# Loading the keys in 256-byte pieces with one PSUM copy per head pair, and issuing a step's V gathers in two halves

## The chip, the core and the metric

The kernel runs on one core of a Trainium2 chip. A core has a matrix engine (TensorE, PE in the profile, with its weight loads shown as PEld), a vector engine (DVE), a scalar engine (ACT), a general engine (POOL) and a sync engine (SP) that computes nothing and issues DMAs. Data lie in HBM, in the on-chip SBUF (128 partitions) and in PSUM, where matmuls write. Sixteen DMA engines move data between HBM and SBUF. Each engine works through its own instruction list in order and waits on semaphores for the others.

The metric is the device time of one launch in microseconds (us). Three executions of the kernel before took 688.04, 689.6 and 687.48 us; the median is 688.04 us.

## The reference

A block-sparse attention (BigBird) feeds a mixture-of-experts layer. B=4 sequences, H=8 heads, S=768 tokens, D=64, blocks of 32 tokens, all float32.

```
scores = q @ k.T / sqrt(D)
mask   = |block_i - block_j| <= 1, or block_i or block_j is first or last,
         or block_j is one of three sampled blocks of block_i
attn   = softmax(where(mask, scores, -1e9)) ; x = attn @ v      # x: 3072 rows of 512
logits = normalize(x) @ normalize(expert_emb).T / tau           # 8 experts
e      = argmax(logits) ; gate = softmax(logits)[e]
out    = gate * (relu(x @ w1[e]) @ w2[e])                       # 512 -> 1024 -> 512
```

## The kernel before

The attention works on chunks of 128 queries of one sequence, 24 in all. Two sequences are handled side by side: chunks 0 to 11 belong to sequences 0 and 1, chunks 12 to 23 to sequences 2 and 3. The loop `for s in range(NCH + 1)` (line 1326) has 25 steps. Step `s` scores chunk `now`, prepares chunk `after`, weighs the values of chunk `last` and turns the output of chunk `past`. The order is written out by hand: every engine receives its instructions in the order of this loop and runs them in that order, so a late instruction holds back everything behind it on its engine.

**Keys.** There are 16 head pairs `g`, four per sequence. `load_k` (line 419) loads one pair, 384 KB. Partition p holds six consecutive tokens of each of the two heads, so one piece of the DMA is 6 x 64 x 4 = 1536 bytes, and one DMA covers the pair. `turn_k` (line 492) turns a pair into the transposed layout `kt` with six TensorE transposes into a PSUM tile `kps` (line 501; a transpose takes two tokens of one head side by side) and four copies to `kt` (line 507), each of 64 partitions x 384 elements, two on DVE and two on ACT. The copies write every second token column. The PSUM pool `big` has two buffers; the score tiles `ac`, `dps` and `bps` use the same two. Pairs 0 to 3 are turned before step 0, pairs 4 to 7 at the end of step 1, pairs 8 to 15 in steps 10, 11 and 12 (table `turning`). In those three steps the copies of sampled key blocks into `kg` (`gather_k`, lines 536 and 540) come after the turned keys. SBUF has six buffers for raw keys; the table `keys_at` says in which step pairs 8 to 15 are loaded.

**Values.** Each chunk needs the V rows of its sampled blocks. `gather_v` (line 462) issues one DMA per sampled block and query block: 12 for a pair of chunks (two sequences side by side), each of 32 rows x 16 heads x 256 bytes, into one of two ring buffers `vg`. They are read by `weigh_far` (line 659). The loads of whole V blocks (`vt`) follow the table `values_at`.

**Queries.** `load_q` (line 410) loads 128 queries of two sequences (512 KB in 256-byte pieces) into one of two buffers; `turn_q` (line 513) transposes one chunk's part.

**SP's queue.** `fetch_all` (line 471) issues the gathers of a step, with one ordinary load ahead of every second gather (line 475 the loads, 477 the gathers), and the loads that remain behind them (479). Rows of finished outputs are written to HBM from the same queue (line 820, `x_dram<-x`), at the start of a later step; the next use of that one of three `x` buffers, in `normalize` (line 698), waits for the write to land. Eight semaphores serve the DMAs of SP and ACT in turn, so an issue waits for the landing of the DMA eight places before it.

After the attention, 25 expert tiles of 128 rows follow (`expert_tile`, lines 1157 and 1170), with the weights loaded by line 1110.

Of the kernel before, what the change touches and what calls it, by code (L numbers as in the profile page):

```python
# [3 lines left out]

# [1 line left out]

# [6 lines left out]
F32 = mybir.dt.float32  # L13
# [7 lines left out]
P = 128  # L21
B, H, S, D = 4, 8, 768, 64
# [3 lines left out]
NC = S // P  # L26
# [28 lines left out]
NS = NCH // DUO  # L55
# [316 lines left out]
def shifts(k, engine, s, c):  # L372

    blocks = blocks_of(c)
    key = engine, s, c
    if key not in k.shift:
        _, values = k.nc.values_load_multi_w_load_instructions(
            k.offset[0:1, s, NG * c + blocks[0]:NG * c + blocks[-1] + 1], engines=(engine,), min_val=0, max_val=S - BLK,
            skip_runtime_bounds_check_because="the block numbers are clamped to the blocks there are")
        if engine == mybir.EngineType.SP and s == NRAND - 1:  # L380
            return list(values)
        k.shift[key] = list(values)
    return k.shift[key]


def pair_chunk(s):

    a, at = divmod(s, NC)
    return a, at if a == 0 else (at + 1) % NC


def place(n):

    a, c = pair_chunk(n // DUO)
    return DUO * a + n % DUO, c, n % DUO


def of_seq(src, a, i=None):

    if i is None:  # L400
        return src[DUO * a:DUO * (a + 1)].rearrange("i h s d -> s (i h) d")
    return src[DUO * a + i].rearrange("h s d -> s h d")


def in_pair(t, i=None):

    return t.rearrange("p i h e -> p (i h) e") if i is None else t[:, i]
# [11 lines left out]
def load_k(k, g):  # L419

    b, j = divmod(g, NPAIR)
    k.raw["k", g] = t = k.kld.tile([P, 2, NC, D], F32, name="kraw", tag="kraw", bufs=6)
    return [(t.rearrange("p h c d -> p h (c d)"), k.k[b, 2 * j:2 * j + 2].rearrange("h (p c) d -> p h (c d)", p=P))]


def load_v(k, a, m, i=None):

    v, src = in_pair(k.vt[m], i), of_seq(k.v, a, i)
    return [(v[rows, :, 0:D], src[lo:lo + rows.stop - rows.start]) for rows, lo in pieces(m)]
# [7 lines left out]
def stack(k, s, i=None):  # L437

    st, (_, c) = k.st_ring[s % 2], pair_chunk(s)
    for half in (1,) if c == 0 else (0, 1):  # L440
        k.nc.scalar.copy(out=st[0:D, half, which(i)], in_=k.vt[c][D * half:D * (half + 1), which(i)])


def stack_ends(k, s, halves, i=None):

    for half in halves:
        k.nc.gpsimd.tensor_copy(out=k.st_ring[s % 2][D:P, half, which(i)], in_=k.vt[0][0:D, which(i)])


def blocks_of(c):  # L450

    return range(2 if c == 0 else 0, NG)
# [9 lines left out]
def gather_v(k, s, i=None):  # L462

    a, c = pair_chunk(s)
    t, src = k.vg_ring[s % 2], of_seq(k.v, a, i)
    for r in range(NRAND):
        for g, shift in zip(blocks_of(c), shifts(k, mybir.EngineType.SP, r, c)):
            yield in_pair(t[r * BLK:(r + 1) * BLK, g], i)[:, :, 0:D], src[bass.ds(shift, BLK)]
# [23 lines left out]
def turn_k(k, g):  # L492

    nc = k.nc
    b, j = divmod(g, NPAIR)
    kt = k.kt[b % 2]
    raw = k.raw.pop(("k", g))
    ps = k.big.tile([P, 2, 512], F32, name="kps", tag="big")
    for h in range(2):
        for m in range(NC // 2):  # L500
            nc.tensor.transpose(ps[:, h, m * P:(m + 1) * P], raw[:, h, 2 * m:2 * m + 2].rearrange("p e d -> p (e d)"),  # L501
                                k.ident)
    for h in range(2):
        to = kt[D * h:D * (h + 1), j, 0:S].rearrange("r (p m e) -> r e m p", m=NC // 2, e=2)
        for e in range(2):
            copy = nc.vector.tensor_copy if e == h else nc.scalar.copy
            copy(out=to[:, e], in_=ps[D * e:D * (e + 1), h, 0:3 * P].rearrange("r (m p) -> r m p", m=NC // 2))  # L507
    if j == NPAIR - 1:
        for i, block in enumerate((NB - 1, 0)):
            nc.scalar.copy(out=kt[:, :, S + i * BLK:S + (i + 1) * BLK], in_=kt[:, :, block * BLK:(block + 1) * BLK])  # L510
# [738 lines left out]
def attention_fast(n, ctx):  # L1249
# [3 lines left out]
    nc = n.nc  # L1253
# [65 lines left out]
    nc.sync.dma_start(n.x_dram[N:N + 1, :], zero)  # L1319

    turning = {10: (8, 9), 11: (10, 11, 12), 12: (13, 14, 15)}
    keys_at = {3: (8,), 4: (9,), 5: (10,), 6: (11,), 7: (12,), 8: (13,), 10: (14, 15)}
    values_at = {7: (0,), 8: (1,), 9: (2,), 11: (3,), 13: (4,), 15: (5,)}
    routed = {TURNS.index(DUO * b + 1) + 2: b for b in range(NS - 1)}
    plan = []
    for s in range(NCH + 1):
        now, after, last, past = (TURNS[i] if 0 <= i < NCH else None for i in (s, s + 1, s - 1, s - 2))
        if s in routed:
            plan = after_step(n, routed[s]) + [p for p in plan if p[0] >= s]

        def planned(half):
            for when, part, what in plan:
                if (when, part) == (s, half):
                    what()

        def keys_gathered():
            if after is not None:
                gather_k(n, after)

        ends = last is not None and place(last)[1] == 0  # L1340
        late_keys = s == 1 or s in turning
        if now is not None:
            score_near(n, now)
            score_far(n, now)
        if not late_keys:
            keys_gathered()
        planned(0)
        if s == 0:
            stack_ends(n, 1, (0, 1), 0)
            stack(n, 1, 0)  # L1350
            near_v(n, 1, range(NG), 0)
        elif s == 2:
            stack_ends(n, 0, (1,), 1)
            stack(n, 0, 1)
            near_v(n, 0, range(NG), 1)
        elif s == 3:
            stack_ends(n, 1, (0, 1), 1)
            stack(n, 1, 1)
            near_v(n, 1, range(NG), 1)
        elif s == 4:  # L1360
            stack_ends(n, 0, (0,))
            stack(n, 2)
        elif s % 2 and 5 <= s < NCH:
            if s // DUO + 1 in (NC, NC + 1):
                stack_ends(n, s // DUO + 1, (0, 1))
            stack(n, s // DUO + 1)
        if last is not None:
            weigh_near(n, last, 0)
        if ends:
            score_ends(n, last, 0)  # L1370
            score_ends(n, last, 2)
        if past is not None:
            turn_x(n, past)
        for g in turning.get(s, ()):
            turn_k(n, g)
        if s in turning:
            keys_gathered()
        for part in range(2):
            if last is not None:
                weigh_far(n, last, part)  # L1380
            if after is not None and part == 0 and not ends:
                turn_q(n, after)
        if ends:
            weigh_ends(n, last, (0, 2))
            score_ends(n, last, 1)
            score_ends(n, last, 3)
            if after is not None:
                turn_q(n, after)
        if past is not None:
            chunk_logits(n, past)  # L1390
        ahead, odd = s // DUO + 1, s % DUO
        loads, gathers = [], ()
        if s in (2, 3):
            loads += load_q(n, s)
        elif s >= 4 and not odd and ahead + 1 < NS:
            loads += load_q(n, ahead + 1)
        if s == 3 or s >= 4 and not odd and ahead < NS:
            gathers = gather_v(n, ahead)
        if s == 3:
            near_v(n, 2, (0, 1))  # L1400
        elif s == 4:
            near_v(n, 2, (2, 3))
            near_v(n, 3, (0, 1))
        elif s > 4 and ahead < NS:
            near_v(n, ahead, (2, 3) if odd else (0, 1))
        for g in keys_at.get(s, ()):
            loads += load_k(n, g)
        for m in values_at.get(s, ()):
            loads += load_v(n, 1, m)
        fetch_all(n, gathers, loads)  # L1410
        if ends:
            weigh_ends(n, last, (1, 3))
        if last is not None:
            weigh_near(n, last, 1)
            normalize(n, last)
        if s == 0:
            build_consts(n)
            next(experts)
        if s == 1:
            for g in range(NPAIR, 2 * NPAIR):  # L1420
                turn_k(n, g)
            keys_gathered()
            next(experts)
            next(experts)
            setup.close()
            n.dp = pool("dp_e", 1)
        if s == NC * (B - 1):
            right.close()
            n.wp = n.wp_ctx.enter_context(n.tc.tile_pool(name="wp", bufs=1, side="right", reuse_waits="tile"))
        planned(1)  # L1430
# [224 lines left out]
```

## Time and profile before

| what | value |
|---|---|
| median of three executions | 688.04 us |
| the profiled execution's own time | 691.25 us |
| its span | 689.5 us |
| mean granted TensorE clock | 0.953 |
| start of step 4, 6, 8 (first score matmul) | 90.58, 107.17, 123.77 us |
| start of step 9, 10, 11, 12, 13 | 141.23, 150.67, 165.95, 188.39, 210.57 us |
| first expert matmul (line 1157) | 322.34 us |
| PE busy | 620.6 us (90%) |
| DMA packets | 166,864, of them 123,176 under 512 bytes |

Times inside the execution are counted from the span's start. The span is what the profile covers; the execution's own time is 1.75 us longer, and 3.2 us above the median of the runs. A group's line gives the source line, engine, operation, output and inputs, shape, count, busy time and mean time of one, then the idle time of the engine before them and what ended most of it. The chain is followed back from the last instruction, at each place to what released it; only work on the chain can shorten the execution directly. The granted clock is 1.00 when TensorE runs at full speed, and it drops in stretches where TensorE idles.

### The profile page before, as it was taken

To read this page: it belongs to the slowest core of one execution; us is meant where nothing else is said; L and a number is where in the kernel's file an instruction comes from. 1 tells how busy PE (TensorE), PEld (TensorE's weight loads), DVE (VectorE), ACT (ScalarE), POOL (GpSimd) and SP (SyncE) were. 2 spreads that over 40 slices of the span, in tenths; PEclk is the share of its full clock that TensorE was granted. 3 is DMA by queue.
4 is the path that set the end of the run, shared out by engine and by line. 5 is a ranking of instruction groups with operands and counts; after the bars stand their busy time and mean duration, and the time that the engine had idled before them with its cause. 6 is when DMAs were issued, how large, how long until landed. Compare 5 with 4: busy or idle time off the path is not lost.

```text
span 689.5 us, 18383 instructions
## 1 busy us (share of the span) xinstructions
PE 620.6 (90%) x7496; PEld 483.9 (70%) x7496; DVE 254.0 (37%) x764; ACT 162.1 (24%) x310; POOL 245.2 (36%) x472
## 2 busy tenths in 40 slices
PE   5493999696677999999999999999999999999996
PEld 3382898596577888888777667766477664776673
DVE  3625456344536667723392111121211212112110
ACT  2434455343544554443000000000000000000000
POOL 1321836253208555412202324432344223442232
PEclk9995999888678999999999999999999999999998
DMA  8972479999529999623999999999899998999811
GB/s 207 190 156 50 90 129 177 187 164 204 73 66 138 142 195 165 166 65 119 392 397 402 401 398 405 366 334 344 314 367 412 391 402 317 375 414 388 315 47 32
DMA packets 166864, 170.58 MB, mean 247 GB/s; under 512 B 123176, under 2 KB 127400, under 8 KB 163954
## 3 DMA queue, kind: packets, MB, share of 16 engines
q1 hardware_dynamic: 159458, 155.35, 77.4%
q0 software_dynamic: 5216, 13.43, 5.4%
q8 instruction: 61, 1.00, 0.7%
q10 hardware_dynamic: 2096, 0.52, 0.4%
q14 instruction: 33, 0.27, 0.1%
HBM read 156.65 MB, written 12.90 MB: 246 GB/s over the span
## 4 chain that ended last, share of the span: by engine, by line
PE 76%; DVE 8%; ACT 5%; DMA 2%; issue 2%; SPq 1%; POOL 0%; DVEq 0%; POOLq 0%; ACTq 0%
PE hp L1157 23%; PE yp L1170 22%; PE av L634 7%; PE dps L579 5%; PE ac L554 3%; PE yp L722 3%; PE ac L557 3%; ACT kt L507 3%; DVE kt L507 2%; PE hp L1202 2%; PE yp L1222 2%; PE xg_ps L518 2%; DMA w<-in_moe_w_dram 2%; DVE xt L713 2%; PE xg_ps L711 1%
## 5 line engine op out<-in xcount | busy, mean ns | idle before, releaser
L1157 PEld LDWEIGHTS hp<-xgt,w 128*128 128x128 f32 x1472 | 167.8, 192 | 11.5 <-issue 10.2
L1157 PE MATMUL hp<-xgt,w 128*128 128x128 f32 x1472 | 169.2, 275 | 0.9 <-DMA w<-in_moe_w_dram 0.9
L1170 PE MATMUL yp<-w,h 128*128 128x512 f32 x368 | 161.9, 592 | 0.0
L1170 PEld LDWEIGHTS yp<-w,h 128*128 128x128 f32 x368 | 68.1, 190 | 76.5 <-issue 75.8
L1081 POOL DMA_INDIRECT xg<-x_dram,quarter x88 | 89.4, 1016 | 32.3 <-issue 27.4
L1160 ACT ACTIVATE h<-hp 128x512 f32<-128x512 f32 x23 | 13.7, 597 | 284.1 <-PE hp L1157 240.4
L1183 POOL DMA_INDIRECT out_dram<-y,slot_l x20 | 20.5, 1026 | 155.8 <-DVE y L1182 155.8
L536 POOL COPY kg<-kt 128x128 f32 x176 | 43.9, 296 | 85.1 <-DVE kt L507 78.6
L1164 DVE TENSOR_SCALAR h<-hp 128x512 f32<-128x512 f32 x23 | 15.9, 691 | 148.3 <-PE hp L1157 148.3
L554 PE MATMUL ac<-qt,kt 128*64 128x128 f32 x352 | 52.1, 309 | 16.5 <-DVE qt L523 14.5
L489 POOL COPY vg<-vt 32x1040 f32<-32x1040 f32 (+1 forms) x45 | 43.1, 957 | 60.5 <-PE av L634 48.4
L554 PEld LDWEIGHTS ac<-qt,kt 128*64 128x64 f32 x352 | 46.1, 159 | 17.8 <-issue 15.7
L557 PE MATMUL ac<-qt,kt 128*64 128x256 f32 (+1 forms) x192 | 51.6, 422 | 3.2 <-ACT kt L510 3.2
L579 PEld LDWEIGHTS dps<-qt,kg 128*64 128x64 f32 x1408 | 50.7, 147 | 2.4 <-issue 2.4
L579 PE MATMUL dps<-qt,kg 128*64 128x64 f32 x1408 | 49.1, 231 | 2.0 <-DVE kg L536 2.0
L1182 DVE TENSOR_SCALAR y<-yp,gate 128x512 f32<-128x512 f32 x20 | 15.0, 750 | 82.0 <-PE yp L1170 69.9
L523 DVE COPY qt<-xg_ps 64x512 f32<-64x512 f32 x48 | 33.1, 689 | 30.7 <-PE xg_ps L518 30.3
L584 ACT ACTIVATE pd<-dps,bias 128x256 f32<-128x256 f32 x88 | 34.7, 475 | 20.2 <-PE dps L579 20.2
L634 PE MATMUL av<-st,pac 128*64 128x65 f32 x704 | 32.0, 233 | 7.0 <-DVE x L811 5.7
L507 DVE COPY kt<-kps 64x384 f32<-64x384 f32 x32 | 26.8, 838 | 29.3 <-ACT kt L507 28.9
L507 ACT COPY kt<-kps 64x384 f32<-64x384 f32 x32 | 26.6, 832 | 29.0 <-DVE kt L507 28.6
L501 PE MATMUL kps<-ident,kraw 128*128 128x128 f32 x96 | 17.7, 341 | 16.6 <-issue 16.6
(229 smaller groups left out, 686.8 us busy)
## 6 DMA issues: line engine op xcount, KB each, us to landing
w<-in_moe_w_dram SPq DMA_DIRECT2D x52, 2048.0 KB
vg<-in_v_dram SPq DMA_DIRECT2D x114, 128.0 KB
kraw<-in_k_dram SPq DMA_DIRECT2D x16, 384.0 KB
x_dram<-x SPq DMA_DIRECT2D x10, 516.0 KB
qraw<-in_q_dram SPq DMA_DIRECT2D x9, 512.0 KB
w<-in_moe_w_dram SPq DMA_DIRECT2D x8, 512.0 KB
vt<-in_v_dram SPq DMA_DIRECT2D x10, 256.0 KB
vt<-in_v_dram SPq DMA_DIRECT2D x5, 512.0 KB
```

The costliest lines, as they stand in the source:

```text
L489: k.nc.gpsimd.tensor_copy(out=k.vg_ring[s % 2][NRAND * BLK:P, g, which(i)], in_=k.vt[m][rows, which(i)])
L507: copy(out=to[:, e], in_=ps[D * e:D * (e + 1), h, 0:3 * P].rearrange("r (m p) -> r m p", m=NC // 2))
L523: k.nc.vector.tensor_copy(out=t[rows, :, h], in_=ps[rows])
L536: copy(out=t[:, :, g, s * BLK:(s + 1) * BLK], in_=kt[:, :, bass.ds(shift, BLK)])
L554: nc.tensor.matmul(out[0:D, j, half], lhsT=kt[:, j, at:at + D], rhs=qt[:, j, :, D * half:D * (half + 1)], start=True, stop=True)
L557: nc.tensor.matmul(out[D:P, j, half:2].rearrange("p f h t -> p h f t"), lhsT=kt[:, j, S:S + D], rhs=qt[:, j, :, D * half:P].rearrange("p h ...
L579: nc.tensor.matmul(out[D * r:D * (r + 1), NG * j + g], lhsT=kg[:, j, g, D * r:D * (r + 1)], rhs=qt[:, j, :, cols], start=True, stop=True)
L584: nc.scalar.activation(e[:, :, g].rearrange("p j h t -> p j (h t)"), out.rearrange("p (j g) h t -> p j g (h t)", g=NG)[:, :, g], ACT.Exp, ...
L634: k.nc.tensor.matmul(av[lanes, h // NPAIR, h % NPAIR * P:h % NPAIR * P + D + 1], lhsT=lhsT, rhs=rhs, start=first[0], stop=last, skip_group ...
L1081: k.nc.gpsimd.indirect_dma_start(out=x[:, g], out_offset=None, in_=quarters, in_offset=bass.IndirectOffsetOnAxis(ap=k.quarter[:, g, t:t + ...
L1157: nc.tensor.matmul(hp[:, f, :], lhsT=w1[:, d, (f0 + f) * P:(f0 + f + 1) * P], rhs=xt[:, d, :], start=(d == 0), stop=(d == ND - 1))
L1170: nc.tensor.matmul(yp, lhsT=h[:, f, :], rhs=w2[:, f, :], start=(f == 0), stop=(f == NF - 1))
```

## The change

A pair of K is loaded by two DMAs, one per head, so that partition p holds tokens p, 128 + p, 256 + p and so on. One piece is then one token of one head, 256 bytes. `turn_k` transposes the two heads of a 128-token chunk together, and the columns arrive in the order that `kt` wants; one copy of 128 partitions x 768 elements replaces the four, on DVE for even and on ACT for odd pairs. The table of K loads starts at step 2 with two pairs and goes on with one per step from 3 to 6; pairs 14 and 15 stay in step 10. From step 4 on an even step issues the first six gathers and the odd step after it the other six; the load of queries moves from the even to the odd step. Step 3's gathers stay whole.

```diff
 def load_k(k, g):
-    k.raw["k", g] = t = k.kld.tile([P, 2, NC, D], F32, name="kraw", tag="kraw", bufs=6)
-    return [(t.rearrange("p h c d -> p h (c d)"), k.k[b, 2 * j:2 * j + 2].rearrange("h (p c) d -> p h (c d)", p=P))]
+    k.raw["k", g] = t = k.kld.tile([P, NC, 2, D], F32, name="kraw", tag="kraw", bufs=6)
+    return [(t[:, :, h], k.k[b, 2 * j + h].rearrange("(c p) d -> p c d", p=P)) for h in range(2)]
...
 def turn_k(k, g):
-    for h in range(2):
-        for m in range(NC // 2):
-            nc.tensor.transpose(ps[:, h, m * P:(m + 1) * P], raw[:, h, 2 * m:2 * m + 2].rearrange("p e d -> p (e d)"),
-                                k.ident)
-    for h in range(2):
-        to = kt[D * h:D * (h + 1), j, 0:S].rearrange("r (p m e) -> r e m p", m=NC // 2, e=2)
-        for e in range(2):
-            copy = nc.vector.tensor_copy if e == h else nc.scalar.copy
-            copy(out=to[:, e], in_=ps[D * e:D * (e + 1), h, 0:3 * P].rearrange("r (m p) -> r m p", m=NC // 2))
+    for c in range(NC):
+        nc.tensor.transpose(ps[:, c // 3, c % 3 * P:(c % 3 + 1) * P], raw[:, c].rearrange("p h d -> p (h d)"), k.ident)
+    copy = nc.scalar.copy if g % 2 else nc.vector.tensor_copy
+    copy(out=kt[:, j, 0:S].rearrange("p (w t) -> p w t", w=2), in_=ps[:, :, 0:3 * P])
...
-    keys_at = {3: (8,), 4: (9,), 5: (10,), 6: (11,), 7: (12,), 8: (13,), 10: (14, 15)}
+    keys_at = {2: (8, 9), 3: (10,), 4: (11,), 5: (12,), 6: (13,), 10: (14, 15)}
...
-        elif s >= 4 and not odd and ahead + 1 < NS:
+        elif s >= 4 and odd and ahead + 1 < NS:
             loads += load_q(n, ahead + 1)
-        if s == 3 or s >= 4 and not odd and ahead < NS:
+        if s == 3:
             gathers = gather_v(n, ahead)
+        elif s >= 4 and ahead < NS:
+            if not odd:
+                coming = gather_v(n, ahead)
+            gathers = coming if odd else islice(coming, 6)
```

More of the change, by code (lines that the diff above doesn't have):

```diff
@@ L2 @@
 from functools import partial
-from itertools import zip_longest
+from itertools import islice
 import dataclasses
```

## The prediction

> **What bounds the kernel now.** I read the chain that ended last first, then the groups, then the chain in order of time, then clock and DMA by stretch, then SP's own queue.
>
> ```profile
> PE 76%; DVE 8%; ACT 5%; DMA 2%; issue 2%; SPq 1%; POOL 0%; DVEq 0%; POOLq 0%; ACTq 0%
> PE hp L1157 23%; PE yp L1170 22%; PE av L634 7%; PE dps L579 5%; PE ac L554 3%; PE yp L722 3%; PE ac L557 3%; ACT kt L507 3%; DVE kt L507 2%; PE hp L1202 2%; PE yp L1222 2%; PE xg_ps L518 2%; DMA w<-in_moe_w_dram 2%; DVE xt L713 2%; PE xg_ps L711 1%
> ...
> L507 DVE COPY kt<-kps 64x384 f32<-64x384 f32 x32 | 26.8, 838 | 29.3 <-ACT kt L507 28.9
> L507 ACT COPY kt<-kps 64x384 f32<-64x384 f32 x32 | 26.6, 832 | 29.0 <-DVE kt L507 28.6
> ```
>
> TensorE bounds most of it, but the key copies (L507) hold 5%, some 34 us. The groups say why: DVE waits for ACT's copy and ACT for DVE's, so the four copies of a pair run one after another, 64 copies, 53.4 us in a row. The chain in time shows it at the end of step 1 (start, duration, what):
>
> ```profile
> 51.84 0.84 DVE kt L507
> 52.69 0.02 issue
> 52.71 0.83 ACT kt L507
> 53.54 0.01 issue
> 53.55 0.83 ACT kt L507
> ...
> 64.68 0.84 DVE kt L507
> ```
>
> Next, stretches: an ordinary step (98.88 on), the step behind a stall, and turning steps 10, 11, 12. Columns: busy time per engine with counts, granted clock, DMA share, GB/s.
>
> ```profile
> 98.88:107.17 8.29, 8.10 (x206) 7.41 (x204) 6.27 (x19) 5.36 (x10) 8.00 (x21) 1.00 1.21 202
> 123.77:141.23 17.46, 11.81 (x206) 10.54 (x204) 5.04 (x20) 3.26 (x8) 3.36 (x8) 0.76 1.00 187
> 150.67:165.95 15.28, 9.75 (x214) 8.82 (x213) 8.93 (x28) 6.85 (x12) 2.10 (x2) 0.92 1.06 197
> 165.95:188.39 22.44, 15.95 (x218) 14.28 (x219) 10.60 (x25) 11.10 (x19) 7.99 (x19) 0.65 0.79 110
> 188.39:210.57 22.18, 14.83 (x219) 13.39 (x219) 10.86 (x27) 8.91 (x16) 3.22 (x10) 0.73 0.43 77
> ```
>
> An ordinary step is full of PE work. The turning steps take two to three times as long and run at a lower clock. The step from 123.77 has another cause, seen in the waits and in SP's issues:
>
> ```profile
> DVE x L698 <- DMA x_dram<-x: 8.1, 1, 8.1
> ...
> SPq L475 <- PE xg_ps L518: 53.7, 8, 18.6
> ...
> 113.48 0.40 SPq L475 DMA_DIRECT2D qraw<-in_q_dram  x1
> 114.13 1.96 SPq L477 DMA_DIRECT2D vg<-in_v_dram  x2
> 116.13 0.49 SPq L475 DMA_DIRECT2D kraw<-in_k_dram  x1
> 116.85 9.38 SPq L477 DMA_DIRECT2D vg<-in_v_dram  x10
> 126.33 1.14 SPq L820 DMA_DIRECT2D x_dram<-x  x2
> ```
>
> The x rows are written behind twelve gathers that leave SP at the DMAs' pace; `normalize` waits 8.1 us for them. Last, the rate of 256-byte packets, in stretches of gathers alone (206 to 216 us) and of whole V blocks (22 to 24):
>
> ```profile
> DMA packets 6566, 1.65 MB, mean 165 GB/s; under 512 B 6565, under 2 KB 6565, under 8 KB 6565
> ...
> DMA packets 1848, 0.47 MB, mean 233 GB/s; under 512 B 1848, under 2 KB 1848, under 8 KB 1848
> ```
>
> **The change part by part.**
>
> *One copy per pair.* No row has a 128x768 copy on DVE. Bounds: 691 ns (128x512, L713) and 2 x 838. The new copy is not strided, so I take the line through 424 ns for 256 elements (L698) and 691 for 512: 0.96 us. ACT: 0.81 us, as its 128x768 reads of PSUM (L603, 809 ns). Even and odd pairs use different engines, so copies now overlap, and the six transposes of a pair set the pace: 1.51 us cold (14.94), 0.75 warm (twelve in 1.50 at 155.55). Transposes keep count and shape.
>
> Pairs 0 to 3: copies run from 11.45 to 25.11. New: pairs 0 and 1 are transposed by 12.5 as now; pair 2 gets its PSUM buffer at 12.4, ends at 13.9, pair 3 at 15.4, its copy at 16.2. Gain 8.9; less 0.5 for the arrival of pair 3 (below): 8.4.
>
> Pairs 4 to 7: 51.84 to 65.52. New: copy of pair 4 until 52.8, two more transposes (2 x 1.5) and a last copy of 0.81: 56.6. Gain 8.9.
>
> Steps 10 to 12: 59.9 us against 3 x 8.3 = 24.9, an excess of 35.0, made of 32 serial copies (27) and the slow clock that the idling brings. What stays: at warm clock two pairs 1.5 of transposes plus a copy of 0.96, 2.5; three pairs wait once for a buffer, about 2 x 0.75 + 2 x 0.96 + 1 = 4.5 each. Sum 11.5, gain 23.5. If the clock stays low, transposes double (+6): 17.5 at worst; 35 at best.
>
> Slow steps after a cold stretch (9: 9.44; 13: 10.34 against 8.3): excess 3.2, I take 2.
>
> *K in 256-byte pieces.* A pair becomes 1536 packets instead of 256. At 233 GB/s its 393 KB take 1.7 us, at 165 GB/s 2.4; the 1536-byte pieces go at about 340 (the stretch from 26 to 28 us, where K alone moves), 1.15. So 0.55 to 1.25 us more per pair, 9 to 20 us of DMA time in all. A destination of 128 partitions is nearer to the V blocks: 0.55. Cover: DMA share is 0.20 from 50 to 75 us, which takes the startup's overrun and pairs 8 and 9; up to 50 us and in steps 3 to 10 the share is about 0.9 and cover thin. I charge 2 us on the path; ends 0 and 20.
>
> [...]
>
> *Sixteen more DMAs on SP.* 0.49 us per issue, 8 us of SP time; SP waits 53.7 us for `turn_q` alone, so 0 on the path, 8 at most. At the start eight DMAs are in flight after pair 1 instead of pair 3: pairs 2 and 3 are issued from 6.57 on (now the time of `vt`, the ninth DMA of SP and ACT together); 786 KB at 233 GB/s take 3.4 us, and behind pair 1 they land at about 12 and 13.5; needed at 12.4 and 13.9. Hence the 0.5; ends 0 and 3. V blocks and gathers queue behind, but step 1 reads them after 40 us.
>
> *Gathers in halves, queries in odd steps.* No instruction is added. The query load now comes after `turn_q` has freed its buffer, so the wait of L475 goes; its queue neighbours leave earlier. The second six gathers are first read two steps later (`weigh_far` in step s+3): 12 us for 5 us of transfer. Ahead of the first x write stand six gathers and pair 13 instead of query, twelve gathers and pair 11: half of 12 us is saved, but K takes 1 to 2 back and the steps before arrive sooner than the queue drains. Of the 8.1 (with cold matmuls 9.2 in that step) I take 4; ends 0 and 9. The second half of step 7 now stands behind the first x write, which waits for the end of step 6 (SP waits 29.9 us in four such cases); if held it leaves later, within its 12 us of room. Late next: V blocks 0 and 1, now among the gathers; they wait for ACT's and POOL's last reads and hold the gathers behind them. POOL issues none of the moved DMAs; its `kg` copies, which wait 78.6 us for keys, start earlier.
>
> *Expert part.* From 322.34 on PE is full and step-bound loads move along: 0.
>
> **Sum**: 8.4 + 8.9 + 23.5 + 2 + 4 - 2 = 44.8. The profiled execution (691.25) would become 646.5; it lies 3.2 above the median, so 688.04 - 44.8 = 643.
>
> **The rivals.**
> A, as summed: 643 (634 to 653). Chance 0.60.
> B, DMA bounds steps 0 to 9: K moves at the gathers' 165 GB/s, 1.25 x 14 pairs = 17.5, of which I let the idle stretch hide 7.5, so 8 beyond the 2 charged; and the x write gains nothing. 643 + 8 + 4 = 655 (to 665). For: share 1.21 in an ordinary step. Against: ordinary steps still take 8.3. Chance 0.24.
> C, second halves late: `weigh_far` waits 2.5 us in each of eight chunk pairs, 20: 663 to 668. For: 165 GB/s. Against: 12 us of room. Chance 0.08.
> D, slower: K's small pieces throttle SP's DMA queue in steps 0 to 10. It takes over once a pair costs 44.8/16 = 2.8 us more on the path, about 3.95 us or 100 GB/s; at 80 GB/s, 4.9 us, the time is 688 + 15 = 703. Against: the slowest saturated stretch shows 165. Chance 0.05.
> E, copies give way to the arrival of keys, nothing is won: 688. Against: copies stand back to back from 51.84, keys long landed. Chance 0.03.
>
> **The numbers.** The likeliest is A: 643. From 630 (no stall at the x write, no DMA cost, the better step 12) to 668, which takes in B and C: about 0.88. Faster by over 0.3% (what a measurement of this kernel tells from none): A, B, C, 0.92; within: E, 0.03; slower: D, 0.05.
>
> **What the profile after would show.** L507: 16 copies, 0.96 and 0.81 us, off the top of the chain. Steps 10 to 12 about 11 to 13 us each at a clock near 1.00. First score matmul of step 2 near 49. The wait of L698 on `x_dram<-x` at half. Steps 3 to 9 at 8.3; if they grow, B or C. Wrong would prove me a DVE copy near 1.7 us, waits of `kps` on `kraw`, or of `av` on `vg`.

## The result, and the profile after

The changed kernel took 645.58 us (median of four executions, 641.01 to 647.52), the kernel before 688.82 us in the four that stand beside them. The ratio is 0.9361, with a 95% interval of 0.9306 to 0.9416: 6.4% faster. Ratios leave out executions more than 1.5% above the fastest of their kernel as slow, which here is one of the four of e4 below (651.79 us). The forecast was 643. The profiled execution after took 645.84 us with a span of 644.0 us, 45.5 us less than the span before; the mean granted clock rose from 0.953 to 0.976.

The chain that ended last, of the kernel after, by engine and by line:

```profile
PE 75%; DMA 7%; SPq 6%; DVE 5%; issue 2%; POOL 2%; ACT 1%; POOLq 0%; DVEq 0%; ACTq 0%
PE hp L1152 25%; PE yp L1165 23%; PE av L629 6%; SPq L477 5%; PE dps L574 4%; PE yp L717 3%; DMA vg<-in_v_dram 3%; PE hp L1197 2%; PE yp L1217 2%; PE ac L549 2%; PE xg_ps L513 2%; PE ac L552 2%; DMA w<-in_moe_w_dram 2%; DMA qraw<-in_q_dram 1%; DMA kraw<-in_k_dram 1%
```

The key copies (now L502) have left the list, where they held 5%. In their place stand transfers: DMA went from 2% to 7%, SP's queue from 1% to 6%, nearly all of it gathers of V (L477). The groups of the key copies after, with their shapes, count, busy time, mean ns, and the idle time ahead of them:

```profile
L502 DVE COPY kt<-kps 128x768 f32<-128x768 f32 x8 | 7.7, 958 | 7.3 <-PE kps L500 7.2
L502 ACT COPY kt<-kps 128x768 f32<-128x768 f32 x8 | 6.4, 796 | 15.3 <-PE kps L500 15.3
```

Sixteen copies take 14.1 us where 64 took 53.4, and they wait for TensorE, no longer for one another. Next the chain in time through the turning of pairs 4 to 7 (start, duration, what):

```profile
41.93 0.97 DVE kt L502
42.90 0.04 issue
42.94 1.54 PE kps L500 x12
44.48 0.02 issue
44.51 0.81 ACT kt L502
```

From the first copy to the end of the last, 3.4 us; before, 13.7. The next table is of stretches: steps 5, 6 and 7, 10 to 12, and 18 and 19 (from:to, length, busy time of PE, PEld, DVE, ACT, POOL with counts, granted clock, DMA share, GB/s).

```profile
78.39:91.13 12.74, 10.56 (x206) 9.40 (x204) 6.27 (x19) 5.35 (x10) 8.17 (x21) 0.85 1.15 163
91.13:100.87 9.74, 9.54 (x205) 8.87 (x204) 5.63 (x23) 3.59 (x9) 2.51 (x8) 0.85 0.94 160
100.87:109.17 8.30, 8.11 (x207) 7.43 (x205) 5.33 (x19) 5.46 (x11) 7.71 (x23) 1.00 1.10 163
...
128.97:138.55 9.58, 9.58 (x214) 8.77 (x214) 6.29 (x24) 4.28 (x9) 1.26 (x2) 1.00 1.19 174
138.55:150.26 11.71, 10.58 (x224) 9.41 (x221) 7.42 (x21) 6.65 (x14) 7.43 (x19) 1.00 1.08 194
150.26:161.80 11.54, 10.60 (x219) 9.46 (x219) 6.86 (x22) 5.59 (x12) 4.59 (x12) 1.00 1.16 168
...
204.94:215.46 10.52, 9.17 (x207) 8.30 (x205) 6.48 (x30) 3.37 (x8) 2.75 (x5) 0.91 1.29 176
215.46:226.11 10.65, 10.46 (x204) 9.78 (x204) 7.20 (x26) 5.58 (x11) 7.00 (x24) 0.77 1.22 174
```

The turning steps 10 to 12 went from 59.9 to 32.8 us, at full clock. But step 5 takes 12.74 and step 6 9.74 us, where both took 8.3 before. The timeline of TensorE shows why step 5 is long (start, duration, line, work, and in brackets the idle time ahead of it):

```profile
83.76 0.27 PE L629 MATMUL av<-vg,pd 128*32 128x65 f32 x2 [0.54 <-DMA vg<-in_v_dram]
84.66 0.27 PE L629 MATMUL av<-vg,pd 128*32 128x65 f32 x2 [0.62 <-DMA vg<-in_v_dram]
85.40 0.27 PE L629 MATMUL av<-vg,pd 128*32 128x65 f32 x2 [0.47 <-DMA vg<-in_v_dram]
```

TensorE takes the gathers of step 3 one by one as they land: two matmuls, then the next gather. The idling is followed by a clock of 0.85 in steps 5 and 6. Of the 4.4 us that step 5 is longer than step 7, half is idle time and half is the clock: its 206 matmuls are busy for 10.56 us, the 207 of step 7 for 8.11. SP's queue shows how late the gathers left (start, duration, work, count):

```profile
61.84 5.12 SPq L479 DMA_DIRECT2D kraw<-in_k_dram  x4
67.62 0.37 SPq L475 DMA_DIRECT2D qraw<-in_q_dram  x1
68.18 3.04 SPq L477 DMA_DIRECT2D vg<-in_v_dram  x2
...
75.23 7.25 SPq L477 DMA_DIRECT2D vg<-in_v_dram  x8
```

Pairs 8 and 9 are issued ahead of step 3's gathers, the last of which leaves at 82.5 us. The two waits that answer to those shown of before (`normalize` on the x write, then what is left of SP's waiting for `turn_q`, now L513; total, times, longest):

```profile
DVE x L693 <- DMA x_dram<-x: 3.2, 1, 3.2
```

```profile
SPq L477 <- PE xg_ps L513: 0.2, 1, 0.2
```

The x wait fell from 8.1 to 3.2 us, and SP's wait of 53.7 us for `turn_q` is down to 0.2.

Where the 45.5 us came from, by the first score matmul of steps 3, 10 and 13, in this execution and in a second profiled one of the same kernel from a later session:

| stretch | before, us | after, us | gain | gain, second execution | forecast |
|---|---|---|---|---|---|
| start to step 3 | 75.60 | 53.16 | 22.4 | 20.7 | 17.3 (8.4 + 8.9) |
| steps 3 to 9 | 75.07 | 75.81 | -0.7 | 1.2 | 3 (x write 4, cold step 9 1, DMA -2) |
| steps 10 to 12 | 59.90 | 32.83 | 27.1 | 26.1 | 23.5 |
| step 13 to the end | 478.93 | 482.20 | -3.3 | -2.2 | 1 |
| all | 689.5 | 644.0 | 45.5 | 45.7 | 44.8 |

The total was met because two errors cancel: the first and third stretch, where the copies were, gave 6 to 9 us more than forecast, and the other two 5 to 8 less. That the total came so close to 643 is luck.

### The profile page after: what moved, and what is told of

Same layout as the page of the kernel before. It is cut to its first block, busy times and chain, and to the rows that moved or that the text cites. A ratio compares the mean times of both kernels' runs of the same rounds, so it can differ in the third digit from the quotient of the medians.

```text
span 644.0 us, 18357 instructions
## 1 busy us (share of the span) xinstructions
PE 607.3 (94%) x7496; PEld 471.4 (73%) x7496; DVE 235.6 (37%) x740; ACT 141.6 (22%) x286; POOL 244.5 (38%) x472
## 2 busy tenths in 40 slices
DMA packets 187599, 170.57 MB, mean 265 GB/s; under 512 B 148008, under 2 KB 148136, under 8 KB 184690
## 4 chain that ended last, share of the span: by engine, by line
PE 75%; DMA 7%; SPq 6%; DVE 5%; issue 2%; POOL 2%; ACT 1%; POOLq 0%; DVEq 0%; ACTq 0%
PE hp L1152 25%; PE yp L1165 23%; PE av L629 6%; SPq L477 5%; PE dps L574 4%; PE yp L717 3%; DMA vg<-in_v_dram 3%; PE hp L1197 2%; PE yp L1217 2%; PE ac L549 2%; PE xg_ps L513 2%; PE ac L552 2%; DMA w<-in_moe_w_dram 2%; DMA qraw<-in_q_dram 1%; DMA kraw<-in_k_dram 1%
## 5 line engine op out<-in xcount | busy, mean ns | idle before, releaser
L1152 PEld LDWEIGHTS hp<-xgt,w 128*128 128x128 f32 x1472 | 167.8, 192 | 11.5 <-issue 10.2
L1155 ACT ACTIVATE h<-hp 128x512 f32<-128x512 f32 x23 | 13.7, 597 | 284.1 <-PE hp L1152 226.6
L489 POOL COPY vg<-vt 32x1040 f32<-32x1040 f32 (+1 forms) x45 | 43.1, 958 | 57.2 <-PE av L629 45.0
L531 POOL COPY kg<-kt 128x128 f32 x176 | 43.2, 291 | 45.5 <-ACT kt L502 38.0
L549 PE MATMUL ac<-qt,kt 128*64 128x128 f32 x352 | 47.0, 290 | 3.3 <-DVE qt L518 3.3
L574 PEld LDWEIGHTS dps<-qt,kg 128*64 128x64 f32 x1408 | 48.2, 142 | 0.8 <-POOL vg L489 0.8
L574 PE MATMUL dps<-qt,kg 128*64 128x64 f32 x1408 | 46.9, 226 | 0.5 <-DVE kg L531 0.5
L552 PE MATMUL ac<-qt,kt 128*64 128x256 f32 (+1 forms) x192 | 46.4, 389 | 0.8 <-ACT kt L505 0.8
L549 PEld LDWEIGHTS ac<-qt,kt 128*64 128x64 f32 x352 | 41.5, 147 | 4.2 <-ACT st L441 1.8
L629 PE MATMUL av<-vg,pd 128*32 128x65 f32 x1408 | 32.4, 225 | 3.5 <-DMA vg<-in_v_dram 2.8
L629 PEld LDWEIGHTS av<-vg,pd 128*32 128x32 f32 x1408 | 23.8, 110 | 12.1 <-issue 8.8
L708 DVE COPY xt<-xg_ps 128x512 f32<-128x512 f32 x24 | 16.6, 690 | 31.8 <-PE xg_ps L706 31.7
```

Of the source, the lines that this page charges most:

```text
L489: k.nc.gpsimd.tensor_copy(out=k.vg_ring[s % 2][NRAND * BLK:P, g, which(i)], in_=k.vt[m][rows, which(i)])
L531: copy(out=t[:, :, g, s * BLK:(s + 1) * BLK], in_=kt[:, :, bass.ds(shift, BLK)])
L549: nc.tensor.matmul(out[0:D, j, half], lhsT=kt[:, j, at:at + D], rhs=qt[:, j, :, D * half:D * (half + 1)], start=True, stop=True)
L552: nc.tensor.matmul(out[D:P, j, half:2].rearrange("p f h t -> p h f t"), lhsT=kt[:, j, S:S + D], rhs=qt[:, j, :, D * half:P].rearrange("p h ...
L574: nc.tensor.matmul(out[D * r:D * (r + 1), NG * j + g], lhsT=kg[:, j, g, D * r:D * (r + 1)], rhs=qt[:, j, :, cols], start=True, stop=True)
L629: k.nc.tensor.matmul(av[lanes, h // NPAIR, h % NPAIR * P:h % NPAIR * P + D + 1], lhsT=lhsT, rhs=rhs, start=first[0], stop=last, skip_group ...
```

## The experiments

The kernels of one session ran on one chip, beside the kernel before: 692.31 us in the first (e1 to e4), 692.72 in the second (e5 to e8), 690.65 in the third (e9, e10, e12 and the changed kernel again). Ratios are to those. For times inside a kernel the table at the end gives the stretches.

**e1: one copy per pair alone.** The kernel before with its 1536-byte pieces and its plan, but one copy per pair. With 1536-byte pieces a transpose of both heads at once is not to be had, so each head of each group of tokens goes through its own matmul against the identity, 12 per pair instead of 6.

```diff
-    for h in range(2):
-        for m in range(NC // 2):
-            nc.tensor.transpose(ps[:, h, m * P:(m + 1) * P], raw[:, h, 2 * m:2 * m + 2]...
...
+    for c in range(NC):
+        for h in range(2):
+            nc.tensor.matmul(ps[D * h:D * (h + 1), c // 3, c % 3 * P:(c % 3 + 1) * P], lhsT=raw[:, h, c], rhs=k.ident, ...)
+    copy = nc.scalar.copy if g % 2 else nc.vector.tensor_copy
+    if g >= 8:      # read PSUM in steps, write kt densely
+        copy(out=kt[:, j, 0:S].rearrange("r (p w m) -> r p w m", w=2, m=3), in_=...("r w (m p) -> r p w m", m=3))
+    else:           # read PSUM densely, write every sixth column of kt
+        copy(out=kt[:, j, 0:S].rearrange("r (p w m) -> r w m p", w=2, m=3), in_=...("r w (m p) -> r w m p", m=3))
```

> Before with one copy per pair and nothing else: 1536-byte pieces in one DMA and the plan of before stay; each pair is turned by twelve 64-column matmuls against the identity (about 1.5 us at full clock instead of 0.75) and one copy of 128x768 whose columns are spread (pairs 0 to 7 write every sixth column, pairs 8 to 15 read PSUM with a stride). Theory (the serial copies cost the time): 8.4 + 8.9 + 23.5 + 2 of the prediction less about 5 for the longer turning and a strided copy of up to 1.5 us: 648 to 656 us, and the x write still makes its wait of about 8 us. Rival (the plan of gathers and loads makes most of the gain): 675 to 685.

Measured: 652.35 us (649.42 to 655.06), ratio 0.9416 (0.9368 to 0.9465). The copy alone brings about 40 us; the x wait stays, at 8.9 us. The two forms of the copy were put in to price the write pattern. The groups of e1, by shape and line (L508 writes every sixth column, L505 writes densely):

```profile
L508 DVE COPY kt<-kps 128x768 f32<-128x768 f32 x4 | 6.2, 1539 | 4.6 <-PE kps L501 4.6
L508 ACT COPY kt<-kps 128x768 f32<-128x768 f32 x4 | 6.1, 1520 | 14.5 <-PE kps L501 14.4
...
L505 DVE COPY kt<-kps 128x768 f32<-128x768 f32 x4 | 3.8, 958 | 5.4 <-PE kps L501 5.4
L505 ACT COPY kt<-kps 128x768 f32<-128x768 f32 x4 | 3.2, 800 | 5.3 <-PE kps L501 5.3
```

The same 98,304 elements take 1.53 us when they are written in steps of 24 bytes and 0.96 or 0.80 when the steps are on the reading side. So the copy of before was dear for two reasons: its write pattern, and the order in which the four copies of a pair ran.

**e2: pieces and copy of the change, plan of before.** The changed kernel with the tables and gathers of before.

```diff
-    keys_at = {2: (8, 9), 3: (10,), 4: (11,), 5: (12,), 6: (13,), 10: (14, 15)}
+    keys_at = {3: (8,), 4: (9,), 5: (10,), 6: (11,), 7: (12,), 8: (13,), 10: (14, 15)}
...
-        elif s >= 4 and odd and ahead + 1 < NS:
+        elif s >= 4 and not odd and ahead + 1 < NS:
             loads += load_q(n, ahead + 1)
-        if s == 3:
+        if s == 3 or s >= 4 and not odd and ahead < NS:
             gathers = gather_v(n, ahead)
-        elif s >= 4 and ahead < NS:
-            if not odd:
-                coming = gather_v(n, ahead)
-            gathers = coming if odd else islice(coming, 6)
```

> The changed kernel with the plan of before (gathers whole on even steps, queries on even steps, K loads from step 3): 256-byte pieces and one copy per pair stay. Theory: the wait for the x write comes back, 8 to 9 us, and the wait for gathers in step 5 shrinks by 3 to 5 because no K stands ahead of them in step 2: 648 to 654. Rival (the plan is needed to hide the small pieces): 658 or more. Rival (the plan does nothing): 645 to 647.

Measured: 651.18 us (650.26 to 652.1), ratio 0.9401 (0.9368 to 0.9434). So pieces and copy together are worth about 41 us. The plan on top of them is worth some 3 us by the ratios (0.9401 against 0.9361), but the two intervals overlap, so that gain is not clear of the noise. Here steps 4 to 7 all take 8.3 us; instead the x wait of step 8 grows to 11.0 us and the turning of step 12 waits for a key load, once for 5.3 us. Steps 3 to 9 take as long as after the change (75.3 and 75.8 us): the delay only falls elsewhere.

**e3: the plan alone.** The kernel before with the tables and gathers of the change (e2's diff the other way round).

> Before with the plan of the changed kernel alone (halves, queries in odd steps, K loads from step 2); 1536-byte pieces and four copies per pair stay. Theory: 4 to 8 us from the x write and nothing else: 680 to 685. Rival (plan makes most): 650 to 665.

Measured: 683.31 us (682.97 to 686.81), ratio 0.9885 (0.9842 to 0.9928), about 8 us. The x wait is gone (step 8: 8.5 instead of 17.5 us). The plan does what it says here, where K moves in 1536-byte pieces and the late start leaves the DMAs time: steps 3 to 9 take 65.6 us at a clock of 1.00.

**e4: copy and plan, 1536-byte pieces.** The changed kernel with `load_k` of before and the matmuls and copies of e1.

> The changed kernel with K in 1536-byte pieces in one DMA per pair and the turning of the copy-only run. Theory (the changed kernel is now held up by DMA time in steps 4 to 8 and 18 to 20, and small K pieces are part of it): 634 to 642, with the waits of TensorE for gathers in steps 5 to 7 gone or halved. Rival (small pieces are hidden, the waits come from the gathers' own order): 645 to 650.

Measured: 647.42 us (641.16 to 651.79), ratio 0.9321 (0.926 to 0.9382). A miss: the theory's 634 to 642 did not come. It is not faster than the change, though K is loaded in large pieces; by itself this leaves open whether the pieces cost nothing or the twelve matmuls cost as much. e10 comes back to that.

**e5: engine by head.** One line of the kernel before: both copies of a head go to the same engine.

```diff
-            copy = nc.vector.tensor_copy if e == h else nc.scalar.copy
+            copy = nc.scalar.copy if h else nc.vector.tensor_copy
```

> Before with one word of the turning changed: both copies of a head go to one engine (head 0 on DVE, head 1 on ACT) instead of crossing; loads, transposes, number and shape of copies and the plan stay. Theory (a pair's copies ran one after another because each waits for the other engine's): two chains of two beside each other, 1.67 us a pair instead of 3.35, about half of the copies' 41 us comes back: 662 to 672. Rival (the number of copies or the PSUM buffers set it, not the crossing): 683 to 689. Second rival (a real order on the tile keeps them serial whatever the engines): 686 to 692.

Measured: 670.05 us (667.59 to 675.33), ratio 0.9684 (0.9607 to 0.976): 22 us for one line, half of what the change brings. The groups of e5:

```profile
L507 DVE COPY kt<-kps 64x384 f32<-64x384 f32 x32 | 26.8, 837 | 6.7 <-PE kps L501 6.2
L507 ACT COPY kt<-kps 64x384 f32<-64x384 f32 x32 | 26.7, 833 | 20.3 <-DVE kt L507 18.4 <-PE av L634 1.0 <-DVE bad_block L354 0.5
```

The copies last as long as before. DVE's idle time ahead of them fell from 29.3 to 6.7 us, but ACT still waits 18.4 us for DVE's copies. The chain of e5 shows why (one pair from DVE's second copy on, then ACT's two; start, duration, what):

```profile
44.85 0.84 DVE kt L507
45.69 0.02 issue
45.71 0.02 ACTq L507
45.72 0.04 issue
45.76 0.82 ACT kt L507
46.58 0.01 issue
46.59 0.83 ACT kt L507
```

ACT's copies of head 1 start only when DVE's copies of head 0 are done, after a semaphore (ACTq L507), although they write other rows of `kt`. So a pair still takes four copies in a row, and within a pair the second rival, an order whatever the engines, holds. What e5 gains is that the engine changes once in a pair and not twice: DVE goes on to the next pair while ACT is at this one (DVE's copies from 13.05 to 14.72 us, ACT's from 13.12 to 14.77). The semaphore shows that the order of copies on two engines within a pair is set in the program. What they share is the PSUM tile and the columns of `kt`; no run tells which of the two the order is for.

**e6: engine by head, and writes in steps of 8 bytes.** e5, with the order of the copy's loops turned so that the innermost step is two columns instead of six.

```diff
-        to = kt[...].rearrange("r (p m e) -> r e m p", m=NC // 2, e=2)
+        to = kt[...].rearrange("r (p m e) -> r e p m", m=NC // 2, e=2)
...
-            copy(out=to[:, e], in_=ps[...].rearrange("r (m p) -> r m p", m=NC // 2))
+            copy(out=to[:, e], in_=ps[...].rearrange("r (m p) -> r p m", m=NC // 2))
```

> As the run before, and the copies run through tokens first, so that they write every second column (8-byte steps) and read PSUM with a stride, instead of every sixth column (24-byte steps). In the copy-only run a 128x768 copy that wrote in 24-byte steps took 1.53 us and one that read PSUM with a stride but wrote densely 0.80 to 0.96. Theory (24-byte steps of the writes halve the copy's rate, strided reads are free): 64x384 falls from 0.83 to 0.55 us if 8-byte steps are free too, a pair 1.1 us, 650 to 658. Rival (any step over 4 bytes costs the same): copies stay at 0.83, 662 to 672.

Measured: 657.36 us (655.62 to 658.78), ratio 0.9485 (0.9424 to 0.9546). The tile of the copies of e6 (shortest, median, longest ns, first and last start):

```profile
L507 DVE COPY kt<-kps x32: 549/556/561, 11.4 to 170.8; 64x384 f32<-64x384 f32 x32
L507 ACT COPY kt<-kps x32: 487/493/534, 12.6 to 172.0; 64x384 f32<-64x384 f32 x32
```

Same elements, same count, 0.56 and 0.49 us instead of 0.83. On DVE that is the dense rate: the line through 691 ns for 512 elements (L713 of before) and 958 for 768 gives 0.557 us for 384, an estimate. Four fifths of the change's gain (0.0515 of 0.0639) is had with the loads, transposes and plan of before.

**e7: e6 with the plan of the change.**

> As the run before with the plan of the changed kernel (halves, queries in odd steps, K loads from step 2): 1536-byte pieces, one DMA per pair, six transposes, four copies by head in 8-byte steps. Theory (DMA time of the small pieces holds the changed kernel up by about 10 us in steps 5 to 7 and 18 to 20): 636 to 644. Rival (small pieces cost nothing on the path): 646 to 655, as its copies are longer than one per pair.

Measured: 652.28 us (647.02 to 654.46), ratio 0.9384 (0.9313 to 0.9454). A miss: it was to come out at 636 to 644, and fell into the rival's 646 to 655. Steps 3 to 9 run without a stall (65.4 us), but the start is 9 us later than after the change, and steps 10 to 12 take 41.9 us against 32.8: two copies per engine and pair (0.56 us each on DVE, 0.50 on ACT) are still longer than the one (0.96 or 0.80).

**e8: pieces of 128 bytes.** The changed kernel, each K load split into two halves of the head's 64 numbers, so four DMAs per pair.

```diff
-    return [(t[:, :, h], k.k[b, 2 * j + h].rearrange("(c p) d -> p c d", p=P)) for h in range(2)]
+    half = D // 2
+    return [(t[:, :, h, half * z:half * (z + 1)], k.k[b, 2 * j + h][:, half * z:half * (z + 1)].rearrange("(c p) d -> p c d", p=P))
+            for h in range(2) for z in range(2)]
```

> The changed kernel with K's pieces halved again: 128 bytes, 3072 packets and four DMAs per pair. Theory (packets, not bytes, set the DMA time, and DMA is what bounds steps 4 to 20 now): 1536 more packets a pair at about 600 to 800 per us are 2 us each, 32 in all, of which some 15 to 25 reach the end: 660 to 672. Rival (K's DMA time is hidden): 645 to 650.

Measured: 659.33 us (658.69 to 660.09), ratio 0.9508 (0.945 to 0.9565), just short of the 660 to 672 expected. By the ratios that is 10 to 11 us above the changed kernel (0.9361, and 0.9345 in the third session); by the medians, which are of different sessions, 13.8. 25,089 packets more (212,688 against 187,599) for the same bytes, but also 32 more DMAs to issue, which no run separates from the packets. SP got the first 16 DMAs of K off in 13.1 us, where after the change the first 8 took 9.9; that speaks against a fixed price per DMA, but does not exclude one. The waits of TensorE in e8:

```profile
PE kps L502 <- DMA kraw<-in_k_dram: 7.7, 6, 2.4
PE xg_ps L515 <- DMA qraw<-in_q_dram: 7.4, 2, 6.3
PE av L631 <- DMA vg<-in_v_dram: 6.4, 7, 2.9
```

After the change itself the same waits are 1.4, 5.8 and 2.8 us. In the profiled executions the loss lies ahead of step 3 (9.8 us), in steps 3 to 9 (2.7) and in steps 10 to 12 (2.5). Queries and gathers, which stand in the same queue as K and are unchanged, are waited for longer as well.

**e9: K loads of pairs 8 to 13 at the steps of before.** The changed kernel with `keys_at` of before (e2's first two lines).

> The changed kernel with the table of K loads of before (pair 8 in step 3 to pair 13 in step 8); halves, queries in odd steps, 256-byte pieces and single copies stay. Theory (the first gathers of step 3 are late in step 5 because the small pieces of pairs 8 and 9 stand ahead of them): steps 5 and 6 fall from 12.7 and 9.7 us to 8.3 to 9.5, some of it is given back in steps 7 to 9 where K now meets V blocks: 640 to 645 beside the changed kernel's 645 to 648 on the same chip. Rival (only the total DMA time counts, order is indifferent): no difference over 0.3%, the waits move to steps 7 to 9.

Measured: 645.81 us (643.57 to 650.99), ratio 0.9348 (0.9312 to 0.9385). The changed kernel in the same session: 645.57, 0.9345 (0.9305 to 0.9385). No difference: the theory's gain in steps 5 and 6 came, and was given back. Steps 4 to 6 now take 8.3 us each, and steps 7 to 9 9.4, 13.7 and 10.7. The stall of steps 5 and 6 moved by two steps, and the time to step 10 stayed (128.97 us, here 129.56).

**e10: dense writes everywhere, 1536-byte pieces, the plan of the change.** e4 with the dense form of the copy for all pairs.

> The run with copies and plan, all pairs copied with dense writes and strided PSUM reads: 1536-byte pieces, one DMA per pair, twelve 64-column matmuls, one copy of 0.80 or 0.96 us, plan of the changed kernel. Theory (DMA time of small pieces is on the path of the changed kernel): start of step 2 two to three us earlier than in that run, 638 to 643, faster than the changed kernel by 0.4 to 1%. Rival (what the pieces win, the longer turning in steps 10 to 12 takes back): same as the changed kernel within 0.3%.

Measured: 644.39 us (641.64 to 650.33), ratio 0.9326 (0.9285 to 0.9366): not to be told from the change. Its copies are as long as the change's (957 and 800 ns), so this is the exchange of 256-byte pieces for six more matmuls per pair (and of two DMAs per pair for one). By stretches: steps 3 to 9 take 70.9 us instead of 75.8, and steps 10 to 12 take 41.2 instead of 32.8. What the large pieces win in the first, the turning loses in the second: its matmuls are busy there for 11.1 us instead of 6.7, 4.4 of the 8.4, and the clock is 0.92 instead of 1.00.

**e12: no K loads for the second half.** The changed kernel without the loads of pairs 8 to 15; `turn_k` takes keys of the first half in their place, so the scores of chunks 12 to 23 are computed with those.

```diff
+    if g >= 2 * NPAIR:
+        k.raw["k", g] = k.kept[2 + (g - 2 * NPAIR) % 6]
+        return []
```

> The changed kernel without the loads of pairs 8 to 15: the raw keys of pairs 2 to 7 that are still in the buffers are turned in their place, so the scores of sequences 2 and 3 use other keys, the work on every engine stays the same, and 3.1 MB of DMA in 256-byte pieces are left out. Theory (DMA time in steps 2 to 12 holds steps 5 to 7 and, through the backlog, 18 to 20): steps 5 and 6 near 8.3, steps 18 and 19 near 8.5: 632 to 638. Rival (those waits come from the release of the gathers' buffers and not from DMA time): 643 to 647.

Measured: 636.21 us (631.87 to 640.14), ratio 0.92 (0.9163 to 0.9236), 9.4 us below the changed kernel of the same session. At the 1.7 to 2.4 us per pair of the prediction eight K loads are 13.6 to 19 us of transfer, an estimate from its rows at 233 and 165 GB/s, so half to two thirds of it lies on the path (e12 also leaves out 16 issues of SP). In the profiled executions 4.9 us of the gain fall in steps 3 to 9 and 5.2 from step 13 on, where no K is loaded in either kernel; the other stretches give 2.3 back.

Steps 3 to 9 side by side, one stretch of each kernel. Before:

```profile
75.60:150.67 75.07, 68.32 (x1581) 62.40 (x1577) 38.34 (x130) 35.99 (x73) 38.10 (x96) 0.93 0.94 160
```

After:

```profile
53.16:128.97 75.81, 68.53 (x1580) 62.27 (x1577) 38.97 (x130) 35.99 (x73) 39.13 (x98) 0.95 0.98 169
```

The plan alone (e3), then no late K loads (e12), then large pieces (e10):

```profile
75.28:140.88 65.60, 64.19 (x1581) 58.50 (x1577) 38.24 (x130) 35.96 (x73) 37.85 (x96) 1.00 0.93 163
```

```profile
53.83:124.71 70.88, 65.66 (x1581) 60.13 (x1577) 39.01 (x130) 35.96 (x73) 39.23 (x98) 0.98 0.97 154
```

```profile
53.05:124.00 70.95, 66.83 (x1580) 60.81 (x1577) 38.81 (x130) 36.23 (x73) 39.02 (x98) 0.98 1.10 181
```

The same 1580 matmuls can be done in 65.6 us when nothing is late (e3, clock 1.00). After the change they take 10 us more. e10 and e12, which ask less of the DMAs, recover half of that each. e3 starts this stretch 22 us later than the change does, which gives its loads that much time.

The stretches of the profiled executions, in us:

| kernel | start to step 3 | steps 3 to 9 | steps 10 to 12 | step 13 to end |
|---|---|---|---|---|
| before | 75.6 | 75.1 | 59.9 | 478.9 |
| after | 53.2 | 75.8 | 32.8 | 482.2 |
| e1, copy | 58.4 | 74.3 | 41.3 | 477.7 |
| e2, pieces and copy | 57.2 | 75.3 | 38.7 | 479.2 |
| e3, plan | 75.3 | 65.6 | 59.3 | 481.0 |
| e5, by head | 64.1 | 74.9 | 48.9 | 479.3 |
| e6, by head, 8 bytes | 61.9 | 72.2 | 41.9 | 478.9 |
| e7, e6 and plan | 62.2 | 65.4 | 41.9 | 483.2 |
| e8, 128 bytes | 62.9 | 78.5 | 35.4 | 481.6 |
| e9, late keys | 55.9 | 73.7 | 32.9 | 482.1 |
| e10, large pieces, plan | 53.0 | 71.0 | 41.2 | 480.8 |
| e12, no late K | 53.8 | 70.9 | 34.5 | 477.0 |

## Why the prediction was right, point by point

**The key copies: right, and under-sized.** That they ran one after another and held the path was right (e1; e5 loosens the order and brings half of the gain), and the guessed durations, 0.96 and 0.81 us, measured 0.958 and 0.796. By step 1 the gain is 9.7 us (forecast 8.4). From there to step 2, pairs 4 to 7 among it, it is 10.7 (forecast 8.9): the step that was too careful took the transposes at the slow 1.5 us a pair, and the chain shows twelve in 1.54. Step 2 is another 2.0 us shorter, which no term had. Steps 10 to 12 gave 27.1 us against 23.5: with the copies short TensorE hardly idled (busy for 30.8 of the 32.8 us), the clock was 1.00 in all three, and the steps took 9.6, 11.7 and 11.5 us, the first below the forecast of 11 to 13. The prediction called the new copy "not strided" and so got its length right; that it was the step of the writes that made the old one dear was seen only in e1 and e6. Steps of 24 bytes cost 1.54 us where dense writes cost 0.96 (128x768 on DVE, e1), and steps of 8 bytes 0.56 where steps of 24 cost 0.83 (64x384 on DVE, e6 and e5).

**The x write: the mechanism right, the size low in its own step.** The wait went from 8.1 to 3.2 us, forecast half; step 8 shortened by 7.2 us, of which 4 were charged, since the cold matmuls went too (clock 0.76 before, 1.00 after).

**K in 256-byte pieces: the term that was mis-sized.** The prediction charged 2 us on the path, because DMA share was 0.20 in the idle stretch from 50 to 75 us. But that stretch was in good part the serial copies: the change removes them, and with them the cover: from 50 to 75 us the share is 0.86 after the change. The 340 GB/s for 1536-byte pieces was read too simply as well: of the 720 packets from 26 to 28 us 311 are under 512 bytes, so K does not move alone there. Steps 3 to 6 gave back 7.8 us, and steps 18 and 19 another 3.7. The stall of steps 5 and 6 is there in the second profiled execution too (13.7 and 9.8 us). Steps 18 and 19 lose only 0.6 us there, and steps 16 and 17 lose 1.8 instead: the place varies from one execution to the next, and what makes these late steps long, when the last K load has long landed, stays open. Three runs price the term. Large pieces (e10) shorten steps 3 to 9 by 4.9 us (3.0 against the second execution). Halving the pieces (e8) costs 10 to 14 us for 25,089 packets, 0.4 to 0.55 us per thousand; at that price the 20,735 packets that the change adds would be 8 to 11 us, an estimate, since nothing shows that the price is the same at both sizes, e8 adds DMAs too, and most of its loss lies ahead of step 3, where the change lost nothing against its forecast. And e12 shows that part of K's transfer time is on the path. So the cost is rather 3 to 11 us than 2 (an estimate from these runs), inside the ends of 0 and 20 that the prediction kept.

**Sixteen more DMAs on SP: open; the arrival of the first pairs: nearly right.** SP's wait for `turn_q` is gone, as forecast. But SP's queue now holds 6% of the chain, and no run separates the number of DMAs from the size of the pieces, so that the issues cost nothing is not shown. TensorE waited 1.2 us for the keys of pair 1, and the copy of pair 3 ended at 17.51 us, 0.8 behind the forecast 16.7 (16.2 and the 0.5 for the arrival). The copies of pairs 0 to 3 thus end 7.6 us earlier, where 8.4 were forecast; the rest of the 9.7 us by step 1 comes in step 0, which no term had.

**Gathers in halves: rival C did not come, a relative of B did.** `weigh_far` waits 2.8 us in six places altogether (4.6 us in seven in the second execution), not 2.5 us in each of eight. Three of the six, 1.6 us, are in step 5 and fall on the gathers of step 3, which the change had not split; the others are in steps 9 and 13. B, DMAs that bound steps 0 to 9, is what the trace shows; its 8 us beyond the 2 charged lie within what the runs show for the DMA. But B also let the x write gain nothing, and it gained. Steps 3 to 9 together ended 3.7 us worse than forecast (1.8 in the second execution).

**Where K's loads stand in the plan: indifferent.** e9 puts them back by one or two steps and changes nothing; what the plan may gain on top of the copy (e2, about 3 us, within the noise) would then come with the halved gathers or the moved load of queries, which no run separates. That the debt only moves was not in the prediction.

**The expert part: right.** From step 23 on the two kernels take 393.6 us each (689.5 - 295.89 and 644.0 - 250.37).

No run is clearly faster than the changed kernel with all the work done; e10 is its equal.

## What to carry to other kernels

A low DMA share in a stretch is no cover for new DMA cost if the change removes that stretch (0.20 before and 0.86 after, from 50 to 75 us): work out the cover from the profile that the change will leave. When a queue of loads is the bound, as in the kernels here with 256-byte pieces, look first whether moving a load within it only moves the stall: steps 3 to 9 took 75.3 us in e2 and 75.8 after the change, and step 10 started at 129.56 us in e9 where it started at 128.97. Before rebuilding a load to make a copy cheap, look at who waits for whom among the copies and at the step of their writes; an exchange of engines and a loop order brought four fifths of this gain (e6, 0.0515 of 0.0639).

## What was not expected of the hardware

- A float32 copy from PSUM to SBUF of 128x768 takes 0.96 us on DVE and 0.80 on ACT when it writes densely, and 1.54 and 1.52 when its writes step by 24 bytes (e1). With steps of 8 bytes 64x384 took 0.56 and 0.49 us (e6), instead of 0.83 on both engines with steps of 24 (e5). Reading PSUM in steps of 512 bytes cost nothing: L505 of e1 is as long as the copy of the change, 0.958 and 0.80 us, that reads it densely.
- Halving K's pieces from 256 to 128 bytes, with the same bytes moved and twice the DMAs, cost 10 to 14 us (e8).
